# A spectral layer's sums and one residual pair moved to GpSimd, with the whole instruction order listed anew

## The chip, the cores and the metric

One NeuronCore of one Trainium2 chip runs the program. The metric is the time of one execution on the device, in microseconds (us). The engines are TensorE (PE in the rows), VectorE (DVE), ScalarE (ACT), GpSimd (POOL) and SyncE (SP), which issues most of the DMAs.

## The reference

The input is x, 2048 rows of 512 numbers. Four blocks follow one another, and each adds to x what it computes from the normalized x.

```python
def _A_ref(x, w_r, w_i):
    X = rfft2(x, axes=(-2, -1)) * (w_r + 1j * w_i)
    return irfft2(X, s=(S, D), axes=(-2, -1))

def _B_ref(x, w_gate, w_up, w_down):
    return ((x @ w_gate) * (x @ w_up)) @ w_down      # 512 -> 1792 -> 512

x = x + _A_ref(_layernorm(x), w_r, w_i)              # layer 0, spectral
x = x + _B_ref(_layernorm(x), w_gate, w_up, w_down)  # layer 0, GLU
x = x + _A_ref(_layernorm(x), w_r, w_i)              # layer 1, spectral
x = x + _B_ref(_layernorm(x), w_gate, w_up, w_down)  # layer 1, GLU
```

## The kernel before

x stays in SBUF as `xs`, 16 tiles of 128 rows by 512 columns. Fourier transforms are matrix products on TensorE, and so are the transposes. The GLU's products run in a rounded fp32 format (fp32r in the rows): each operand is a high part, which ScalarE copies, and a low part, what the copy lost, which mostly GpSimd subtracts.

**Spectral layer.** `fwd` (line 556) normalizes a tile, transposes it (`tp`), transforms the columns (`dp`) and begins the rows (`sp`), and ScalarE writes the result into E. `middle` (line 636) works through 16 groups of 512 spectral numbers. For a group VectorE transposes E into T, TensorE finishes the row transform (`zp`), ScalarE makes the rotated copy `jz` in two halves, VectorE multiplies `zp` by the real weights, GpSimd multiplies `jz` by the imaginary weights, somebody adds the two products into `ys`, TensorE begins the way back (`yp`), ScalarE copies into T, and VectorE transposes back into E. The tuples PE_ADDS and POOL_ADDS (lines 71 and 72, one entry for each layer) say who adds: in groups 2, 6, 8, 10 and 14 TensorE, which multiplies both products and accumulates; in all the others VectorE, from PSUM.

`inv` (line 717) brings a tile back: TensorE computes `vp` in two halves, ScalarE copies it to `vs`, TensorE computes `yi`, and the residual is added to xs. In the mode "plain" VectorE does that from PSUM in one pass of 512 columns and two of 256. MODES (line 79) gives one mode for each of the first four pairs of tiles, (0, 4), (1, 5), (2, 6) and (3, 7).

**Crossing to the GLU.** After both tiles of a pair have their statistics, ScalarE normalizes them (`xn`), TensorE transposes them (`tq`), and `build_x` (line 787) makes the seven left operands: XA, three blocks, and XS, four sums of blocks. For the first and third pair VectorE makes the sums; for the second and fourth GpSimd does, four subtractions or additions on the scratch `sx` or `sw`. The four low parts of XS are GpSimd's for every pair. The first products of the GLU (`unit`, line 932) are made over the first two pairs alone: `gw`, `gx`, `gy`, `gx`, `gz`, `gv`, `gz`; `gw` reads the first XS block, `gy` the second, `gz` the third, `gv` the fourth.

**GLU.** `unit` makes seven products for each of 14 column blocks of the weights, and `down` (products `ex` to `ev`) or `db` brings them back to 512 columns and into xs. From the second half of layer 0 on, the weights come from DRAM through DMAs that GpSimd issues (`kept_weights`, line 854: `wt<-gu`).

**Order.** Nothing is emitted where the code stands. Each instruction is first recorded by `plan.op`, which numbers it; `Plan.order` then sorts all of them, and they are emitted in that order, with each engine keeping it (`tc.keep_in_program_order`, in the helper that all rows name as line 411). So an engine takes its instructions strictly in the planned order, and one that waits holds up what stands behind it. Before the change, a list scheduler (`run`) picked by due times, and 277 stored random draws (MOVES) shifted these due times. `Plan.order` also says which buffer of a ring a tile gets.

Of the kernel before, what the change touches and what calls it, by code (L numbers as in the profile page):

```python
# [26 lines left out]
def consts():  # L27
# [44 lines left out]
POOL_ADDS = (), ()  # L72
# [6 lines left out]
MODES = ("plain", "plain", "plain", "fold"), ("plain", "plain", "plain", "fold")  # L79
# [6 lines left out]
MOVES = (  # L86
# [32 lines left out]
RATE = 270.0  # L119
WARM = 2  # L120
EARLY = 0
HOLD, FAR = {"DVE": 1.0, "ACT": 1.0, "POOL": 1.0}, 15.0
CLEAR = 1.5
FREE = ("a", "f", "st", "s1", "s2", "s3")
LOOK, SLACK = 0.08, 20.0
SLOTS = 5
WOVEN, WEND = 8, 20
STO, FRM = 10, 10
DOWNS8 = (7, 8, 11, 12, 15, 16, 19, 20)
DOWNS4 = (8, 12, 16, 20)  # L130
# [18 lines left out]
class Draw:  # L149
# [12 lines left out]
    def one(self, of):  # L162
        return of[int(self.part() * len(of))]
# [1113 lines left out]
```

## Time and profile before

| | us |
|---|---|
| median of 3 runs | 1087.72 (1087.59 to 1087.82) |
| the profiled execution | 1087.75 |
| its span, first to last instruction | 1086.0 |
| TensorE busy in the span | 1072.3 |
| VectorE, GpSimd, ScalarE busy | 841.1, 731.8, 457.7 |
| granted TensorE clock, mean | 1.000 |

Matmuls are pipelined and their ends are modelled, so a matmul's length in a row overlaps the next one; the distance from start to start is what TensorE takes for it.

### The profile page before, as it was taken

The numbers are of one execution on the slowest core, as the hardware profiler recorded it, in microseconds if no ns is written. First come the engines' busy times: TensorE is split into PE (matmuls) and PEld (weight loads), VectorE is DVE, ScalarE is ACT, GpSimd is POOL, SyncE is SP. The second block draws the span as 40 slices with busy tenths as digits, with TensorE's granted clock in tenths as the row PEclk, the third lists the DMA queues.
The fourth block names the chain that finished last, engine by engine and source line by source line (L and its number), as shares of the span: only waits on it lengthen the run. The fifth ranks groups of instructions, "written<-read, shape, count | busy, mean of one in ns | idle before, by whom it ended". The sixth has DMA issues, their size and how long they took to land.

```text
span 1086.0 us, 18629 instructions
## 1 busy us (share of the span) xinstructions
PE 1072.3 (99%) x6500; PEld 923.2 (85%) x6500; DVE 841.1 (77%) x1684; ACT 457.7 (42%) x1045; POOL 731.8 (67%) x940
## 2 busy tenths in 40 slices
PE   8999999999999999999999999999999999999998
PEld 6748988888899988888996489889989998888887
DVE  8597877777877875766897979777897876677778
ACT  6787643344542323323347775223442521223231
POOL 7396799978898666456674527466656984667771
PEclk9999999999999999999999999999999999999999
DMA  7665267556563457454454312655456256556542
GB/s 282 234 213 175 64 223 242 199 204 203 214 223 117 166 182 235 155 165 147 136 199 151 136 54 103 207 168 180 155 175 204 69 175 242 186 184 203 194 137 78
DMA packets 50301, 189.49 MB, mean 174 GB/s; under 512 B 5280, under 2 KB 19104, under 8 KB 39200
## 3 DMA queue, kind: packets, MB, share of 16 engines
q0 software_dynamic: 16128, 102.77, 28.8%
q1 hardware_dynamic: 33792, 85.01, 22.2%
q8 instruction: 52, 0.85, 0.3%
q10 hardware_dynamic: 288, 0.52, 0.1%
q14 instruction: 41, 0.34, 0.1%
HBM read 145.56 MB, written 42.73 MB: 173 GB/s over the span
## 4 chain that ended last, share of the span: by engine, by line
PE 89%; DVE 5%; issue 2%; ACT 2%; POOL 1%; DMA 0%; DVEq 0%; POOLq 0%; ACTq 0%
PE gx L411 14%; PE gz L411 14%; PE db L411 7%; PE gw L411 7%; PE gv L411 7%; PE gy L411 7%; PE ex L411 5%; PE ez L411 5%; PE yi L411 3%; PE ey L411 3%; PE ew L411 3%; PE ev L411 3%; PE sp L411 2%; PE dp L411 2%; PE vp L411 2%
## 5 line engine op out<-in xcount | busy, mean ns | idle before, releaser
L411 PE MATMUL gx<-xA,wt 128*128 128x512 f32 (+1 forms) x852 | 180.8, 347 | 0.0
L411 PEld LDWEIGHTS gx<-xA,wt 128*128 128x128 f32 x852 | 136.9, 190 | 17.2 <-ACT s L411 0.2
L411 DVE TENSOR_TENSOR q<-gy,s 128x512 f32<-128x512 f32 (+1 forms) x71 | 41.1, 578 | 73.4 <-PE gy L411 55.9
L411 ACT CAST sf<-q 128x256 fp32r<-128x256 f32 x99 | 40.2, 406 | 136.5 <-DVE q L411 84.0
L411 POOL TENSOR_TENSOR sf<-q,sf 128x256 fp32r<-128x256 f32 x99 | 73.6, 745 | 31.8 <-ACT sf L411 28.1
L411 DVE TENSOR_TENSOR xs<-xs,db 128x512 f32<-128x512 f32 x128 | 85.6, 683 | 11.4 <-PE db L411 11.0
L411 PE MATMUL db<-wd,h 128*128 128x512 f32 x336 | 91.1, 395 | 0.0
L411 POOL DMA_DIRECT2D wt<-gu x72 | 40.3, 560 | 74.7 <-PE gz L411 48.1
L411 PE MATMUL gz<-xA,wt 128*128 128x512 f32 (+1 forms) x426 | 90.1, 347 | 0.0
L411 PE MATMUL gw<-xS,wt 128*128 128x512 f32 (+1 forms) x426 | 90.0, 347 | 0.0
L411 PE MATMUL gv<-xS,wt 128*128 128x512 f32 (+1 forms) x426 | 90.0, 347 | 0.0
L411 PE MATMUL gz<-xS,wt 128*128 128x512 f32 (+1 forms) x426 | 89.8, 346 | 0.0
L411 PE MATMUL gy<-xS,wt 128*128 128x512 f32 (+1 forms) x426 | 89.7, 346 | 0.0
L411 POOL TENSOR_TENSOR sf<-cc,sf 128x256 fp32r<-128x256 f32 x99 | 73.2, 740 | 21.1 <-ACT sf L411 20.7
L411 PEld LDWEIGHTS gz<-xA,wt 128*128 128x128 f32 x426 | 69.1, 189 | 9.4
L411 PEld LDWEIGHTS gw<-xS,wt 128*128 128x128 f32 x426 | 68.8, 189 | 9.3 <-issue 0.3
L411 PEld LDWEIGHTS gy<-xS,wt 128*128 128x128 f32 x426 | 68.7, 190 | 9.0 <-issue 0.3
L411 PEld LDWEIGHTS gz<-xS,wt 128*128 128x128 f32 x426 | 68.8, 190 | 8.9
L411 PEld LDWEIGHTS gv<-xS,wt 128*128 128x128 f32 x426 | 68.5, 190 | 8.9 <-issue 0.3
L411 ACT COPY s<-gx 128x512 f32<-128x512 f32 (+1 forms) x71 | 35.3, 497 | 92.7 <-PE gx L411 80.7
L411 PEld LDWEIGHTS db<-wd,h 128*128 128x128 f32 x336 | 60.3, 189 | 10.3
L411 ACT CAST sf<-cc 128x256 fp32r<-128x256 f32 x99 | 40.1, 405 | 66.4 <-PE ez L411 22.3
(171 smaller groups left out, 2667.1 us busy)
## 6 DMA issues: line engine op xcount, KB each, us to landing
wt<-gu POOLq DMA_DIRECT2D x36, 1024.0 KB, 5.3
wt<-gu POOLq DMA_DIRECT2D x36, 768.0 KB, 4.7
bf<-dn POOLq DMA_DIRECT2D x20, 1024.0 KB, 5.5
bf<-dn POOLq DMA_DIRECT2D x20, 768.0 KB, 4.6
gu<-wt SPq DMA_DIRECT2D x14, 1024.0 KB, 6.9
gu<-wt SPq DMA_DIRECT2D x14, 768.0 KB, 3.5
wq<-in_wf_dram SPq DMA_DIRECT2D x10, 1024.0 KB, 6.1
rg<-in_wb_dram SPq DMA_DIRECT2D x14, 512.0 KB, 4.8
```

The lines of the kernel that those rows point to most:

```text
L411: ins = f(*args, **kw)
```

## The change

Two settings of layer 1 change. In groups 5, 9 and 13 of `middle` the two products are added by GpSimd: VectorE writes its product to SBUF instead of PSUM, and a GpSimd pass of 512 columns takes the place of one on VectorE. For the third pair (tiles 2 and 6) the mode is "pool": ScalarE copies `yi` to SBUF (`yc`), and GpSimd adds it to xs in four passes of 256 columns for each tile, in place of VectorE's three. TensorE's instructions stay the same 1200 blocks.

The scheduler with its draws is gone. A list ORDER of all 5057 instruction numbers gives the order; `Plan.order` walks it, and only keeps account of buffers. The order differs from the old one on every engine but the two first ScalarE loads, in both layers.

Numbers of the list used here. Layer 0: 603, 601 are the transposes (`tq`) of the second pair, 605 to 608 ScalarE's copies of them, 609 to 612 GpSimd's sums; 551, 549 the transposes of the first pair; 637, 627, 679, 847 are column transforms (`yi`); 844, 845, 878, 879, 857, 858 row transforms (`vp`) of later tiles; 736, 735 the GLU's first `gx` and `gw`. Layer 1: 2961, 2999, 3038 are the three sums of `middle`; 3146, 3144 the transposes of the second pair, 3149, 3150 ScalarE's first copies of them, 3152 to 3155 GpSimd's sums, 3159, 3161, 3163, 3165 the low parts of that pair's four XS blocks, 3105, 3107, 3109, 3111 those of the first pair; 3182 and 3170 are `yi` of tiles 6 and 2, 3183 and 3171 the copies `yc`, 3184 to 3187 and 3172 to 3175 the GpSimd passes; 3284, 3287 the first `gw` and `gy`; 3590, 3591 weight fetches of the third column block. Start: 5, 7, 8 are loads of x, 24 and 42 of row tables.

```diff
-POOL_ADDS = (), ()
+POOL_ADDS = (), (5, 9, 13)
...
-MODES = ("plain", "plain", "plain", "fold"), ("plain", "plain", "plain", "fold")
+MODES = ("plain", "plain", "plain", "fold"), ("plain", "plain", "pool", "fold")
...
-MOVES = (
-    1200000011, 1200000042, 1200000094, 1200000106, 1200000108, 1200000117, 1200000161, 1200000172, 1200000175,
...
+ORDER = (
+    0, 6, 5, 24, 42, 4, 7, 15, 1, 60, 78, 8, 9, 10, 13, 2, 11, 25, 18, 26, 3, 19, 20, 27, 43, 21, 36, 22, 44, 28, 23,
...
+    521, 592, 539, 693, 593, 694, 327, 597, 594, 326, 598, 329, 599, 595, 676, 596, 602, 522, 677, 600, 695, 603, 328,
+    523, 696, 678, 601, 605, 524, 634, 606, 697, 635, 607, 877, 525, 608, 625, 609, 698, 604, 624, 856, 526, 636, 610,
+    614, 679, 330, 613, 540, 615, 611, 541, 637, 619, 542, 545, 626, 616, 546, 547, 543, 680, 544, 617, 620, 681, 550,
+    627, 682, 618, 638, 548, 1087, 331, 612, 683, 699, 513, 639, 551, 621, 684, 700, 549, 640, 622, 701, 516, 628, 844,
+    552, 685, 845, 554, 629, 500, 553, 878, 501, 502, 555, 641, 890, 911, 879, 630, 556, 561, 857, 642, 559, 846, 562,
+    858, 565, 560, 736, 557, 880, 566, 702, 643, 735, 703, 558, 686, 737, 1034, 847, 563, 644, 567, 687, 645, 704, 564,
+    631, 741, 859, 632, 705, 568, 738, 848, 709, 706, 646, 710, 707, 647, 711, 708, 881, 651, 648, 714, 739, 652, 649,
+    860, 712, 1157, 650, 740, 715, 653, 849, 742, 656, 850, 1210, 851, 718, 744, 719, 743, 717, 852, 713, 721, 747, 745,
...
+    2958, 2977, 2987, 2952, 2959, 2943, 2978, 2970, 2915, 2953, 2988, 2960, 3003, 2994, 2979, 2971, 2961, 3021, 3022,
+    3033, 2996, 3011, 2980, 2995, 2989, 3050, 3034, 2962, 2997, 3035, 2923, 2990, 2998, 2981, 3036, 2963, 2933, 2999,
+    3004, 2944, 2991, 3042, 3037, 3012, 2964, 3005, 3023, 2972, 3014, 3038, 3006, 3043, 3013, 2954, 3024, 3051, 3007,
...
+    3075, 3135, 3180, 3136, 3064, 3076, 3181, 3427, 3140, 3077, 3141, 3078, 3142, 3137, 3138, 3167, 3139, 3145, 3065,
+    3168, 3079, 3143, 3223, 3081, 3066, 3224, 3448, 3067, 3169, 3146, 3068, 3080, 3182, 3069, 3149, 3150, 3082, 3083,
+    3225, 3152, 3144, 3084, 3183, 3239, 3088, 3089, 3151, 3090, 3184, 3085, 3086, 3170, 3093, 3087, 3153, 3240, 3158,
+    3241, 3185, 3091, 3226, 3242, 3186, 3148, 3243, 3171, 3162, 3157, 3187, 3227, 3415, 3244, 3147, 3172, 3094, 3228,
+    3188, 3245, 3416, 3229, 3173, 3449, 3097, 3156, 3246, 3174, 3450, 3230, 3092, 3189, 3247, 3154, 3249, 3417, 3191,
+    3231, 3095, 3175, 3098, 3418, 3160, 3232, 3102, 3104, 3155, 3248, 3428, 3099, 3159, 3429, 3164, 3100, 3285, 3190,
+    3250, 3163, 3101, 3233, 3106, 3161, 3110, 3192, 3286, 3234, 3096, 3176, 3105, 3251, 3290, 3430, 3103, 3107, 3252,
+    3177, 3284, 3193, 3256, 3108, 3111, 3257, 3287, 3194, 3258, 3253, 3419, 3254, 3261, 3109, 3255, 3198, 3431, 3199,
+    3259, 3200, 3195, 3165, 3288, 3262, 3196, 3289, 3203, 3291, 3197, 3420, 3265, 3293, 3421, 3266, 3201, 3292, 3268,
...
+    3334, 3321, 3323, 3359, 3441, 3361, 3453, 3325, 3360, 3335, 3336, 3379, 3590, 3326, 3362, 3328, 3364, 3327, 3442,
+    3363, 3330, 3337, 3365, 3324, 3445, 3443, 3446, 3367, 3331, 3444, 3447, 3454, 3366, 3338, 3591, 3455, 3368, 3329,
...
     def order(self, hop=0.12):
 
-        ops = self.ops
+        ops, out, rings, free, bus, port = self.ops, [], {}, {}, 0.75, 0.0
...
-        out, marks = self.run([], [])
-        for n in MOVES:
-            out, marks = self.run(out, *self.move(n, out, marks)[:1])
-        return out
...
+        for o in (ops[n] for n in ORDER):
+            e = o["e"]
+            at = max([self.after_(ops[p], o) for p in o["pre"]] + [free.get(e, 0.75), port if o["two"] else 0.0])
```

The branches that the two settings choose stand in the kernel already:

```python
                elif where == "POOL":
                    pool(512, lambda q=q, y=y: gtt(y(), y(), q(), ALU.add), [y, (q, 0), (q, 1)], [y])
...
        if mode == "pool":
            yc = temp("yc", "f")
            act(512, lambda: A.copy(yc(), yi()), [yi], [yc])
            y4 = lambda: yc().rearrange("p (b a d) -> p b a d", a=2, b=2)
            for b in range(2):
                pool(256, lambda b=b: gtt(xt[:, b], xt[:, b], y4()[:, 0], ALU.add), [yc, x_], [x_], due=due)
                pool(256, lambda b=b: gtt(xt[:, b], xt[:, b], y4()[:, 1], (ALU.add, ALU.subtract)[b]), [yc, x_], [x_])
```

## Rows read from the trace of the kernel before

**Rows 1.** The page, busy time of TensorE's matmuls, share of the span, instructions
```profile
PE 1072.3 (99%) x6500; PEld 923.2 (85%) x6500; DVE 841.1 (77%) x1684; ACT 457.7 (42%) x1045; POOL 731.8 (67%) x940
```

**Rows 2.** The page, the chain that ended last, by engine
```profile
PE 89%; DVE 5%; issue 2%; ACT 2%; POOL 1%; DMA 0%; DVEq 0%; POOLq 0%; ACTq 0%
```

**Rows 3.** Windows: stretch, then length and busy time of each engine (instructions), clock, DMA
```profile
0.00:60.00 60.00, 55.10 (x359) 39.77 (x360) 43.34 (x127) 42.37 (x105) 32.64 (x47) 1.00 0.71 251
...
90.00:130.00 40.00, 38.41 (x282) 36.08 (x282) 35.20 (x108) 32.34 (x87) 24.01 (x33) 1.00 0.33 113
130.00:556.00 426.00, 426.00 (x2498) 374.07 (x2498) 318.75 (x599) 152.25 (x331) 320.55 (x386) 1.00 0.55 185
...
600.00:620.00 20.00, 20.00 (x48) 8.66 (x47) 20.00 (x35) 15.84 (x28) 13.07 (x12) 1.00 0.31 104
620.00:650.00 30.00, 28.62 (x181) 24.94 (x180) 23.96 (x68) 20.53 (x54) 6.38 (x9) 1.00 0.20 65
...
680.00:1086.00 406.00, 401.89 (x2513) 362.42 (x2511) 309.57 (x538) 123.82 (x281) 256.23 (x359) 1.00 0.52 171
```

**Rows 4.** Timeline of TensorE, 570:680: start, length, instructions, [idle before, releaser]
```profile
589.78 3.70 PE L411 MATMUL zp<-T,midt 128*128 128x512 f32 x8 [0.62 <-DVE T L411]
...
624.90 2.18 PE L411 MATMUL vp<-tw,E 128*128 128x128 f32 x16 [0.28 <-DVE E L411]
...
637.98 1.06 PE L411 MATMUL yi<-di,vs 128*128 128x128 f32 x8
638.88 0.60 PE L411 MATMUL tq<-ident,xn 128*128 128x128 f32 x4
...
641.09 3.72 PE L411 MATMUL yi<-di,vs 128*128 128x256 f32 x16 [0.68 <-ACT vs L411]
645.23 0.66 PE L411 MATMUL tq<-ident,xn 128*128 128x128 f32 x4 [0.42 <-ACT xn L411]
...
651.61 0.96 PE L411 MATMUL gy<-xS,wt 128*128 128x256 f32 x6
...
653.13 1.05 PE L411 MATMUL yi<-di,vs 128*128 128x128 f32 x8
653.93 0.96 PE L411 MATMUL gz<-xS,wt 128*128 128x256 f32 x6
...
655.09 0.96 PE L411 MATMUL gv<-xS,wt 128*128 128x256 f32 x6
...
678.93 1.32 PE L411 MATMUL gw<-xS,wt 128*128 128x512 f32 x5
```

**Rows 5.** Groups of VectorE (DVE) in 585:660: busy, mean ns, idle before
```profile
L411 DVE TENSOR_TENSOR ys<-zp,jz 128x512 f32<-128x512 f32 x11 | 7.3, 666 | 0.0
L411 DVE TENSOR_TENSOR xs<-xs,yi 128x256 f32<-128x256 f32 x18 | 7.2, 415 | 0.1
L411 DVE TENSOR_TENSOR xs<-xs,yi 128x512 f32<-128x512 f32 x9 | 6.1, 682 | 4.3 <-PE yi L411 4.2
```

**Rows 6.** The tile jz on GpSimd (POOL), 585:625: ns min/median/max, first and last start
```profile
L411 POOL TENSOR_TENSOR jz<-jz,wr x8: 1266/1271/1277, 597.6 to 612.1; 128x512 f32<-128x512 f32 x8
```

**Rows 7.** Timeline of GpSimd, 586:700
```profile
643.17 3.15 POOL L411 TENSOR_TENSOR sw<-sw 128x256 f32<-128x256 f32 x4 [23.61 <-issue]
...
648.61 2.82 POOL L411 TENSOR_TENSOR xS<-sw,xS 128x256 fp32r<-128x256 f32 x4 [0.22 <-ACT xS L411]
...
667.40 0.59 POOL L411 DMA_DIRECT2D wt<-gu  x1 [0.54 <-PE gy L411]
```

**Rows 8.** Groups of ScalarE (ACT) in 620:655
```profile
L411 ACT COPY vs<-vp 128x512 f32<-128x512 f32 x11 | 6.1, 586 | 2.1 <-PE vp L411 2.1
```

**Rows 9.** Timeline of TensorE, 70:140
```profile
104.36 0.66 PE L411 MATMUL tq<-ident,xn 128*128 128x128 f32 x4 [1.16 <-ACT xn L411]
...
109.71 1.16 PE L411 MATMUL yi<-di,vs 128*128 128x128 f32 x8 [0.43 <-ACT vs L411]
```

**Rows 10.** Timeline of GpSimd, 60:125
```profile
103.73 3.15 POOL L411 TENSOR_TENSOR sx<-sx 128x256 f32<-128x256 f32 x4 [8.52 <-ACT sx L411]
```

More of the change, by code (lines that the diff above doesn't have):

```diff
@@ L121 @@
 EARLY = 0
-HOLD, FAR = {"DVE": 1.0, "ACT": 1.0, "POOL": 1.0}, 15.0
 CLEAR = 1.5
-FREE = ("a", "f", "st", "s1", "s2", "s3")
-LOOK, SLACK = 0.08, 20.0
 SLOTS = 5
@@ L146, in __call__ @@
         return self.tile
-class Draw:
-    def __init__(self, seed):
-        self.at = seed * 0x9E3779B97F4A7C15 % 2 ** 64
-    def part(self):
-        self.at = (self.at + 0x9E3779B97F4A7C15) % 2 ** 64
-        z = self.at
-        z = (z ^ z >> 30) * 0xBF58476D1CE4E5B9 % 2 ** 64
-        z = (z ^ z >> 27) * 0x94D049BB133111EB % 2 ** 64
-        return ((z ^ z >> 31) >> 11) * 2.0 ** -53
-    def one(self, of):
-        return of[int(self.part() * len(of))]
-    def bell(self):
-        return (self.part() + self.part() + self.part() + self.part() - 2.0) * 1.7320508
 class Plan:
@@ L174 @@
              **{f"{r}{p}": n for p in range(4) for r, n in (("s", SLOTS),)}}
-    FREE = FREE
     def __init__(self):
@@ L213, in order @@
             o["due"] = d - 1.1 * o["lag"] - hop - 0.3 * (o["e"] == "PE")
-        self.kinds = [(o["e"], *(t.name for t in o["tiles"])) for o in ops]
-        out, marks = self.run([], [])
-        for n in MOVES:
-            out, marks = self.run(out, *self.move(n, out, marks)[:1])
-        return out
-    def move(self, n, out, marks):
-        ops, draw = self.ops, Draw(n)
-        end = max(o["end"] for o in out)
-        lo, span = -20.0 + draw.part() * (end + 10.0), draw.one((10.0, 20.0, 40.0, 80.0, 160.0))
-        share, jit, way = draw.one((0.0, 0.25, 0.5, 1.0)), draw.one((0.0, 0.0, 2.0, 5.0)), draw.part()
-        inside = [o for o in ops if lo < o["start"] < lo + span]
-        if way < 0.4 and inside:
-            kind, by = self.kinds[draw.one(inside)["i"]], 8.0 * draw.bell()
-            for o in inside:
-                if self.kinds[o["i"]] == kind:
-                    o["due"] += by
-        elif way < 0.7 and inside:
-            for _ in range(1 + int(3.0 * draw.part())):
-                draw.one(inside)["due"] += 8.0 * draw.bell()
-        elif inside:
-            self.latest(out, end)
-            shifts = sorted(o["late"] - o["due"] for o in inside)
-            shift = shifts[len(shifts) // 2]
-            for o in inside:
-                o["due"] += share * (o["late"] - shift - o["due"]) + jit * draw.bell()
-        return [m for m in marks if m[1] < lo - 15.0], lo + span
@@ L244, in latest @@
-    def latest(self, out, end):
-        ops = self.ops
-        nxt, two = {}, None
-        for o in reversed(out):
-            long = o["end"] - o["start"]
-            late = end - long
-            for s in o["suc"]:
-                late = min(late, ops[s]["late"] - (0.0 if ops[s]["next_to"] is o else long))
-            if o["e"] in nxt:
-                late = min(late, nxt[o["e"]] - o["pitch"])
-            if o["two"]:
-                if two is not None:
-                    late = min(late, two - o["pitch"])
-                two = late
-            for t in o["tiles"]:
-                if t in self.after:
-                    late = min(late, self.after[t]["late"] - long)
-            nxt[o["e"]] = late
-            o["late"] = late
+        for o in ops:
+            for t in o["tiles"]:
+                t.left, t.slot, t.freed = t.users, None, 0.0
@@ new lines, in order @@
+        for o in (ops[n] for n in ORDER):
+            e = o["e"]
+            at = max([self.after_(ops[p], o) for p in o["pre"]] + [free.get(e, 0.75), port if o["two"] else 0.0])
+            if e == "SP":
+                at = max(at, o["due"] - o["ahead"])
+            for t in o["tiles"]:
+                if t.slot is None:
+                    t.slot = True
+                    q = rings.setdefault(t.ring, [])
+                    t.index = len(q)
+                    if len(q) == self.RINGS.get(t.ring, 1):
+                        old = min((u for u in q if not u.left), key=lambda u: u.freed)
+                        at = max(at, old.freed)
+                        q.remove(old)
+                        t.index = old.index
+                    q.append(t)
+            o["start"] = at
+            free[e] = at + o["pitch"]
+            if o["two"]:
+                port = at + o["pitch"]
+            if o["kb"]:
+                bus = max(bus, at) + o["kb"] / RATE
+                o["end"] = max(at + o["lag"], bus + 2.3)
+            else:
+                o["end"] = at + o["lag"] + hop + 0.3 * (e == "PE")
+            for t in o["tiles"]:
+                t.left -= 1
+                t.freed = max(t.freed, o["end"])
+            out.append(o)
```

104 lines of the change are left out of this document (removed), and 264 rows, old and new, of tables (MOVES, ORDER).

## The prediction

> **What bounds the kernel now.** I read the page's busy times first, then its chain, then windows by stage, then the timelines where windows leave TensorE idle. The reader should see in [rows 1] that TensorE is busy for 1072.3 of 1086.0 us, and in [rows 2] that 89% of the chain that ended last is TensorE's own work. The change removes no work from TensorE, so it can gain only what TensorE waits. The windows place these waits [rows 3]: 4.9 us in the first 60, 1.6 in 90 to 130 where layer 0 crosses from its spectral part to the GLU, none in 130 to 556, 1.4 in 620 to 650 where layer 1 crosses, and 4.1 after 680, most of it the tail of additions and stores after the last product. Between 680 and the tail TensorE does not wait, so what is gained or lost before 680 arrives at the end in full.
>
> In layer 1 two things stand side by side. From 600 to 620 VectorE is busy 20.00 of 20 us, and so is TensorE [rows 3]; relief for VectorE alone is worth only the small holes of TensorE. And at the crossing TensorE stops three times, 0.28, 0.68 and 0.42 us, on VectorE's transpose, ScalarE's copy and ScalarE's normalizing [rows 4]. GpSimd, which gets the work, stood still for 23.61 us until 643.17 [rows 7]. In layer 0 the same crossing has stops of 1.16 and 0.43 us [rows 9], and GpSimd begins its sums at 103.73 after 8.52 us of nothing [rows 10].
>
> The sum below is made against the profiled execution, 1087.75 us (span 1086.0 and 1.75 around it); the median, 1087.72, is the same within the spread.
>
> **1. Three sums in layer 1's middle.** Removed from VectorE: 3 passes of 0.666 us [rows 5], about 0.6 from start to start, so 1.8. Added to GpSimd: 3 passes; a product of the same shape takes 1.27 us [rows 6], so 3.8 in a stretch where GpSimd worked 13.07 of 20 [rows 3]. ScalarE is not touched. What does it buy? TensorE's stretch from the first `zp` at 589.78 to the stop at 624.90 [rows 4] lasts 35.1 us. Its own work there is 16 `zp`, 16 `yp` and 5 second `yp`, 37 blocks; 8 instructions in 3.70 us put a block of two at about 0.86, 31.8 in all; with four `vp` blocks of 0.5 (16 instructions in 2.18) and the small product, 33.9. So 1.2 us are waiting. VectorE, full throughout, would end 1.8 us sooner, TensorE can end 1.2 sooner at best. I take 1.0, as the first turns of the stage are not helped; bounds 0 (GpSimd's sums, in series behind its products, come late) and 1.2. **-1.0**
>
> Does moving work from VectorE to GpSimd slow either? [Rows 6] shows GpSimd's products at 1.266 to 1.277 us in the stretch where VectorE was full, so in that traffic neither blocked the other. The Trainium skill has a rule against such a change: Perfetto Trace Analysis, "Optimizing Scalar/DVE Operations", says that the two share an SBUF read port, so that moving work between them might not help. SBUF — State Buffer, "Who interferes with whom", narrows it to VectorE instructions with two SBUF inputs, which VectorE's work here mostly isn't (one input is in PSUM). By the row the sum stands; by the first rule terms 1 and 2 would be zero.
>
> **2. The third pair on GpSimd, and layer 1's crossing.** VectorE loses, for two tiles, one pass of 0.682 and two of 0.415 each [rows 5], 3.0 us by duration, some 2.5 from start to start. ScalarE gains two copies of 0.586 [rows 8], 1.2 us, in a window where it has 9.5 free [rows 3]. GpSimd gains 8 passes; four of that shape took 2.82 us, 0.70 each [rows 7], 5.6 in all. Behind them in GpSimd's queue stand the low parts that the GLU's first products need. In the new list I count the GpSimd instructions from 3152: `gw` needs 3105, the 16th, `gy` 3107, the 17th, and the last low part, 3165, is the 20th; before, they were 12.
>
> When can 3152 start? It started at 643.17 because ScalarE made its copies late. The list puts 3149 and 3150 right behind the transposes; the earlier one ran at 637.98 + 0.90 = 638.88 at the latest [rows 4], so some 639. After it GpSimd waits for tile 6: `yi` 1.8 us (half of 3.72 [rows 4]), the copy 0.59, so about 641. From there 16 instructions of 0.70 to 3107: 652.1, and 1.0 less for term 1: 651.1. `gy` started at 651.61 before [rows 4]. Without its stops TensorE would be there some two us sooner, so GpSimd, not VectorE, sets this point, and only 0.3 to 0.5 us come on top of term 1. I take 0.3. Bounds: a gain of 1.1 (both later stops gone), a loss if 3152 cannot start early (the slow rival). **-0.3**
>
> The weight fetch 3590 stood 24 instructions behind 3152 and was issued at 667.40 [rows 7]; it now stands 40 behind. 40 of 0.70 are 28 us: 667 from a start at 639, perhaps 671 with waits, landing some 5 us later (the queue's median on the page). TensorE needs it at 678.93 [rows 4], or about 677.5 now. That covers it by a little; I take nothing, bound 3 us of loss.
>
> **3. Layer 0's crossing, order alone.** Before, the transpose that waited 1.16 us for its normalized tile stood ahead of `yi` 627, and `yi` 847 waited 0.43 [rows 9]. In the list 603 and 601 come before the last `vp` blocks, ScalarE's copies 605 to 608 directly behind, 637 and 627 ahead of 551 and 549 together, six `vp` blocks after these, and 847 behind the first `gx` and `gw`. So 1.8 us of ready work fills the first stop, the second loses its place, and GpSimd's sums, which set the low parts, can start perhaps 1.5 us before 103.73 [rows 10]. The two stops are 1.6 us; I take 1.5; bounds 0 and 2.0. **-1.5**
>
> **4. Everything else in the order.** The first 60 us have 4.9 us idle [rows 3], of which the first load and the first statistics are no matter of order. The list also sends loads 24 and 42, 128 KB each, ahead of load 7; 256 KB at the 251 GB/s of that window [rows 3] is 1.0 us by which tiles 2 and 3 can be late. Gain bound 2.5, loss bound 1.0. I take 0.8 over all other stages, since the list moves blocks at nearly every small hole I looked at. **-0.8**
>
> **5. Kinds of neighbours on TensorE.** A `yi` block of 8 took 0.90 us when a fp32 transpose followed (637.98 to 638.88) and 0.80 when a fp32r product followed (653.13 to 653.93) [rows 4]. The list has, net, nine fewer short blocks (`tp`, `yi`, `vp`, `tq`) followed by fp32r: 9 × 0.09 = 0.8. Some stand where TensorE waits anyway; I take 0.6; bounds 0 and 0.9. **+0.6**
>
> Sum: 1087.75 - 1.0 - 0.3 - 1.5 - 0.8 + 0.6 = 1084.75, so **1084.8 us**, 0.27% faster.
>
> **Rivals.**
>
> *The gains don't add up (no measurable change).* In both crossings GpSimd's low parts take over as what ends last; the holes merely move. For it: GpSimd's chain grows from 12 to 20 instructions, and in layer 0 it is as long as before. Then terms 1 to 3 give perhaps 1.4 together, terms 4 and 5 cancel: 1086.4. The shared-port rule ends in the same place: terms 1 and 2 gone, 1086.1.
>
> *Slower: GpSimd's chain starts no earlier than before.* If the copies ahead of 3152 still wait for VectorE, 3152 starts at 643.17; at the 0.79 of the four sums there (3.15 us [rows 7]) 17 instructions end at 656.6, 5.0 us after the old `gy`. Term 1 is lost too: 1087.75 + 5.0 - 1.5 - 0.8 + 0.6 = 1091.1. It begins to cost from a start of about 640 on, and outweighs the rest from about 642. Against it: GpSimd's long rest, and the list's order on ScalarE. A fetch 3590 that lands after 678 is the same mechanism one stage later.
>
> *More than forecast.* The new order removes most of what is removable: both stops of layer 0, all three of layer 1 and 2.5 at the start: 1087.75 - 1.2 - 1.1 - 2.0 - 2.5 + 0.4 = 1081.4.
>
> **Chances.** A measurement of this kernel tells 0.2%, 2.2 us, from no change. The forecast case, 2.2 to 4.5 us faster, 0.45; more than that 0.10; within 2.2 us 0.33; slower by more 0.12. So faster 0.55, same 0.33, slower 0.12. The range leaves out some 0.06 below and 0.13 above: **1082.0 to 1089.0**. The likeliest case alone is 1083.3 to 1085.5.
>
> **What would show it.** Right: VectorE still full in the middle but ended about 1.8 us sooner, the first `yi` of layer 1 about 1 us sooner; GpSimd at work from about 639 on, its low parts ending just ahead of `gw` and `gy`; no stop of over 0.5 us between 100 and 112; TensorE's busy blocks 1200 as before; DVE instructions 9 fewer. Wrong: TensorE waiting on GpSimd's `xS` at `gw` or `gy`, or on a DMA at the third column block; a stop of tile 2's transpose in the first 12 us; or new holes between 680 and 1080, where today there are none and where the order was changed as well.

## The result, and the profile after

The changed kernel took 1091.07 us (median of 8 runs, 1089.40 to 1091.59), the kernel before on the same chip 1087.92 (8 runs, 1087.26 to 1088.80). The ratio is 1.0025, with a 95% interval of 1.0015 to 1.0036: slower by about a quarter of a per cent. Forecast were 1084.8 and a range of 1082.0 to 1089.0; the time lies above it. The profiled execution took 1090.86 us, its span is 1089.1, the mean granted clock 0.998. Five of the eight executions have that mean clock and took 1090.86 to 1091.59; the three with 0.999 or 1.000 took 1089.40 to 1089.84, which is above the range too.

The page of after, busy times and chain, answers to [rows 1, 2]:

```profile
PE 1074.9 (99%) x6500; PEld 925.9 (85%) x6500; DVE 837.4 (77%) x1675; ACT 458.1 (42%) x1047; POOL 741.6 (68%) x951
...
PE 80%; POOL 7%; DVE 3%; issue 2%; ACT 2%; DMA 0%; POOLq 0%; DVEq 0%; ACTq 0%
```

Nine DVE instructions went, eleven came to GpSimd, as announced. TensorE is busy 2.6 us longer with the same 6500 matmuls, and the chain leads through GpSimd for 7% of the span, before for 1%. The windows, in the order of [rows 3]:

```profile
0.00:60.00 60.00, 54.46 (x351) 40.11 (x352) 40.53 (x122) 40.75 (x99) 30.13 (x44) 0.97 0.67 243
90.00:130.00 40.00, 39.70 (x289) 37.50 (x288) 35.24 (x108) 34.81 (x94) 26.89 (x36) 1.00 0.50 168
130.00:556.00 426.00, 424.79 (x2476) 372.37 (x2475) 316.60 (x593) 151.49 (x330) 320.66 (x387) 1.00 0.54 185
600.00:620.00 20.00, 19.82 (x46) 8.38 (x45) 20.00 (x36) 15.88 (x31) 16.89 (x16) 1.00 0.37 131
620.00:650.00 30.00, 29.80 (x175) 24.77 (x173) 22.31 (x59) 21.31 (x53) 10.09 (x15) 1.00 0.24 75
680.00:1089.10 409.10, 404.90 (x2532) 365.11 (x2531) 311.63 (x543) 123.49 (x282) 257.42 (x361) 1.00 0.52 171
```

The two windows of the crossings are nearly free of TensorE's waits now (0.30 of 40 and 0.20 of 30 us, against 1.6 and 1.4; layer 1's has moved out of its window in part, see below), and GpSimd took up the work of layer 1 (16.89 us busy from 600 to 620 against 13.07). What the windows show as new: eight matmuls fewer in the first 60 us, a clock of 0.97 there, and 1.2 us of waiting in 130 to 556, where there was none.

A window does not say when time is lost, since its edges are fixed. For that, the start of TensorE's n-th matmul is taken from both traces; the difference is how late the changed kernel is at that point. Matmuls are counted from 0. Where the order of blocks differs locally, a single value can be off by up to 1 us: it is 1.17 at no. 1380 and 0.24 at no. 1400, though nothing is gained between; where both run like blocks it is steady, 1.30 from 1000 to 1140 and 2.33 at 1560, 1580, 1620 and 1640. Layer 0's start ends ahead of no. 500, its crossing lies between 500 and 700, layer 1's middle between 3400 and 3600, its crossing between 3600 and 3900.

| TensorE's matmul no. | 300 | 500 | 700 | 1400 | 1600 | 3000 | 3400 | 3600 | 3900 | last |
|---|---|---|---|---|---|---|---|---|---|---|
| starts before, us | 45.7 | 97.9 | 125.6 | 267.3 | 306.3 | 529.1 | 578.2 | 626.7 | 668.8 | 1081.5 |
| changed kernel, late by | 2.02 | 3.14 | 1.01 | 0.24 | 2.66 | 2.36 | 3.34 | 2.93 | 2.80 | 3.10 |

So the loss comes ahead of layer 1's middle: 3.1 us at the start, 1.35 between nos. 700 and 3000 (1.0 of it between the steady values), 1.0 between 3000 and 3400. The crossing of layer 0 gave back 2.1 (1.8 by the steady value behind it). Layer 1, where GpSimd's new work is, gained 0.4 in its middle; the 0.1 at its crossing is less than a single value can tell. Each place can be seen in timelines. TensorE's waits between 9 and 60 us, then the first of them as it was before:

```profile
9.01 1.33 PE L487 MATMUL dp<-df,fs 128*128 128x128 f32 x8 [1.41 <-DVE fs L487]
31.87 1.16 PE L487 MATMUL dp<-df,fs 128*128 128x128 f32 x8 [0.64 <-DVE fs L487]
52.63 2.84 PE L487 MATMUL zp<-T,midt 128*128 128x512 f32 x6 [1.58 <-DVE T L487]
58.66 1.55 PE L487 MATMUL yp<-ys,midt 128*128 128x512 f32 x3 [0.38 <-DVE ys L487]
```

```profile
8.61 1.16 PE L411 MATMUL dp<-df,fs 128*128 128x128 f32 x8 [1.07 <-DVE fs L411]
```

The first line waits for VectorE's `fs`, and on VectorE a statistic of the next tile waits for its load ahead of that `fs`; the load stands behind two tables in SP's queue and is issued at 2.12 us. Before, it stood ahead of them (the last line here), and the statistic did not wait:

```profile
2.12 0.43 SPq L487 DMA_DIRECT2D xs<-in_x_dram  x1
...
7.93 0.69 DVE L487 BATCH_NORM_STATS2 st<-xs 128x6 f32<-128x512 f32 x1 [0.84 <-DMA xs<-in_x_dram]
8.54 0.41 DVE L487 TENSOR_TENSOR fs<-tp,fb 128x256 f32<-128x256 f32 x1
...
0.75 0.86 SPq L411 DMA_DIRECT2D xs<-in_x_dram  x2
```

The wait is only 0.34 us longer than before. But behind it TensorE's granted clock falls from 2.4 to 1.2 GHz for 3.4 us (0.50 in the third column from the right); before, it stood at 1.00 there (the last line), and 25 matmuls ran in the 3 us instead of 16:

```profile
9.00:10.00 1.00, 0.99 (x8) 0.99 (x9) 0.96 (x5) 0.00 (x0) 1.00 (x2) 0.93 0.95 344
10.00:13.00 3.00, 3.00 (x16) 2.77 (x17) 2.96 (x12) 1.84 (x7) 3.00 (x5) 0.50 1.03 414
13.00:14.00 1.00, 1.00 (x8) 0.70 (x8) 0.96 (x4) 0.68 (x1) 0.96 (x2) 0.86 1.01 414
...
10.00:13.00 3.00, 3.00 (x25) 2.33 (x25) 2.96 (x8) 2.38 (x6) 2.68 (x5) 1.00 1.03 406
```

At 52.63 the first turn (the first transposes of E into T) is late. One reading: the list has ScalarE copy the second piece of E ahead of the rest of the first, and VectorE's transposes begin with one that reads both. The run first_turn, below, does not bear this out, and the cause inside the first turn stays open. Another candidate in the trace, which no run tries by itself: ScalarE's last two `us` of this stage start at 47.22 and 48.17 now and at 45.02 at the latest before, and the copies into E follow them. The same transposes began at 48.77 before, while TensorE still had row products (`sp`) to do (the last two lines):

```profile
50.04 1.43 ACT L487 COPY E<-sp 128x257 f32<-128x257 f32 x6 [0.20 <-PE sp L487]
...
51.28 1.90 DVE L487 STREAM_TRANSPOSE T<-E 128x512 f32<-128x512 f32 x3 [5.23 <-ACT E L487]
...
48.77 2.49 DVE L411 STREAM_TRANSPOSE T<-E 128x512 f32<-128x512 f32 x4 [8.91 <-ACT E L411]
...
48.57 0.92 PE L411 MATMUL sp<-us,tw 64*128 64x193 f32 x8 [0.40 <-ACT E L411]
```

At 273 us the rounded copies `u` of kept weights are stored to DRAM (`dn`) from two buffers of the ring that the GLU's temporaries use. The stores were issued at 258.68 before (the last line) and at 267.67 now, where they land 4.5 us after their issue; the next users of these buffers, a sum `c` on VectorE and `xn` on ScalarE, wait for them, and `gz` behind `c`:

```profile
267.67 1.02 SPq L487 DMA_DIRECT2D dn<-u  x2
...
272.30 0.69 DVE L487 TENSOR_TENSOR c<-gz,q 128x512 f32<-128x512 f32 x1 [1.85 <-DMA dn<-u]
...
273.04 1.20 PE L487 MATMUL gz<-xA,wt 128*128 128x512 f32 x4 [0.85 <-DVE c L487]
...
258.68 1.04 SPq L411 DMA_DIRECT2D dn<-u  x2
```

What is lost between nos. 3000 and 3400 is lost at one place: the kernel is 2.25 us late at no. 3060 and 3.22 at 3080. VectorE's `q` waits 1.38 us there for GpSimd's `cc`, and two products of TensorE wait behind VectorE. Each wait reads 0.18, but from the start of the matmul ahead to the start of the second one behind it pass 0.68 and 0.65 us, where two others take 0.24; that is 0.85 of the 0.98.

```profile
538.69 0.43 DVE L487 TENSOR_TENSOR q<-gy,s 128x256 f32<-128x256 f32 x1 [1.38 <-POOL cc L487]
...
539.17 0.98 PE L487 MATMUL gz<-xS,wt 128*128 128x256 f32 x6 [0.18 <-DVE q L487]
540.32 0.95 PE L487 MATMUL ez<-bf,sf 128*128 128x256 f32 x6 [0.18 <-DVE ew L487]
```

Layer 1 on TensorE, for [rows 4], and GpSimd, for [rows 7]:

```profile
593.29 4.56 PE L487 MATMUL zp<-T,midt 128*128 128x512 f32 x10 [0.63 <-DVE T L487]
...
626.03 3.98 PE L487 MATMUL vp<-tw,E 128*128 128x128 f32 x32
...
650.04 1.16 PE L487 MATMUL yi<-di,vs 128*128 128x128 f32 x8 [0.24 <-ACT vs L487]
...
653.73 0.98 PE L487 MATMUL gx<-xA,wt 128*128 128x256 f32 x6 [0.88 <-ACT s L487]
654.54 0.88 PE L487 MATMUL gw<-xS,wt 128*128 128x256 f32 x6
655.26 0.88 PE L487 MATMUL gy<-xS,wt 128*128 128x256 f32 x6
```

```profile
641.95 0.72 POOL L487 TENSOR_TENSOR sw<-sw 128x256 f32<-128x256 f32 x1 [18.87 <-issue]
...
651.36 5.62 POOL L487 TENSOR_TENSOR xS<-sw,xS 128x256 fp32r<-128x256 f32 x8
...
674.29 0.57 POOL L487 DMA_DIRECT2D wt<-gu  x1
```

The stretch from the first `zp` to the first `vp` takes 32.74 us. GpSimd's first sum starts at 641.95, which is 639 on the old clock of events (TensorE is 2.9 late there), as forecast. The stops of 0.68 and 0.42 us are gone; a new one of 0.88 came, of the second `gx` on a copy of the first.

### The profile page after: what moved, and what is told of

Its sections match the earlier page's. It is cut to its first block, busy times and chain, and to the rows that moved or that the text cites. A ratio compares the mean times of both kernels' runs of the same rounds, so it can differ in the third digit from the quotient of the medians.

```text
span 1089.1 us, 18620 instructions
## 1 busy us (share of the span) xinstructions
PE 1074.9 (99%) x6500; PEld 925.9 (85%) x6500; DVE 837.4 (77%) x1675; ACT 458.1 (42%) x1047; POOL 741.6 (68%) x951
## 4 chain that ended last, share of the span: by engine, by line
PE 80%; POOL 7%; DVE 3%; issue 2%; ACT 2%; DMA 0%; POOLq 0%; DVEq 0%; ACTq 0%
PE gx L487 13%; PE gz L487 13%; PE gy L487 7%; PE gv L487 6%; PE gw L487 6%; PE db L487 5%; PE ex L487 5%; PE ez L487 5%; PE ey L487 3%; PE ev L487 3%; PE yi L487 2%; PE ew L487 2%; PE yp L487 2%; PE vp L487 2%; POOL wt L487 2%
```

## The experiments

OLD is the list of the kernel before in the new numbers, with the added GpSimd work where the replaced instructions stood; NEW is the changed list. `OLD[:k] + NEW` means OLD's first k entries, then all others in NEW's order. Every kernel but old_settings has the changed settings. Times are medians, with the median of the kernel before beside them and the ratio's 95% interval.

**The halves.** What belongs to layer 1, and what to the settings?

```diff
-ORDER = NEW
+ORDER = OLD[:2900] + NEW   # layer1_new: layer 0 as before
+ORDER = OLD                # old_order_new_settings
```

> Old order up to layer 1's first transpose E to T (2900 instructions), from there on the changed kernel. Theory A: the middle of layer 1 gains about 0.5 us and nothing is lost before it: about 1087.4 (1086.8 to 1088.0). Theory B: 1089.5 or more.

> The two settings alone, with the old order of all instructions (a GpSimd pass stands where the VectorE pass stood). Theory A: the settings cost little, 1087.5 to 1089. Theory B: GpSimd's passes delay the low parts of layer 1's crossing, 1090 or more, with TensorE waiting for xS near 651.

layer1_new took 1087.20 against 1087.63 (0.9988 to 1.0005): the 3 us are gone, so they came from the order of the first 2900 entries, which is all that differs. A gain over the kernel before is not clear of noise. old_order_new_settings took 1095.62 against 1087.63 (1.0058 to 1.0084). With the old order GpSimd's passes stand where VectorE's did, `gw` waits for its low part, and the clock falls with it, to 0.50 for 6.8 us:

```profile
656.67 1.44 PE L490 MATMUL gw<-xS,wt 128*128 128x256 f32 x5 [4.25 <-POOL xS L490]
```

The opposite kernel has the new order without the new GpSimd work:

```diff
-POOL_ADDS = (), (5, 9, 13)
+POOL_ADDS = (), ()
-MODES = ("plain", "plain", "plain", "fold"), ("plain", "plain", "pool", "fold")
+MODES = ("plain", "plain", "plain", "fold"), ("plain", "plain", "plain", "fold")
```

> The changed list with what GpSimd does anew undone: the three sums back on VectorE, the third pair's residual passes as before (the list less the operations that exist only in the new form). Theory A (the new GpSimd work gains 1.0 in layer 1's middle and nothing at its crossing): 0.6 to 1.6 us more than the changed kernel, 1091.7 to 1092.7. Rival B (it gains nothing, layer 1's 0.6 comes from the order): 1091.

1093.91 against 1087.81 (1.0046 to 1.0072), 2.8 us more than the changed kernel and more than either theory had. Its layer 1 has two stops that the changed one does not have (what ends the second, the profile does not show), and the one at the second `gx` takes 1.05 instead of 0.88:

```profile
617.93 1.12 PE L489 MATMUL zp<-T,midt 128*128 128x512 f32 x2 [1.17 <-DVE ys L489]
649.90 0.71 PE L489 MATMUL vp<-tw,E 128*128 128x128 f32 x4 [2.43 <-issue]
656.79 0.97 PE L489 MATMUL gx<-xA,wt 128*128 128x256 f32 x6 [1.05 <-ACT s L489]
```

**The start.**

```diff
-ORDER = NEW
+ORDER = OLD[:302] + NEW               # start_old
+ORDER = OLD[:335] + NEW               # start_old_all
+ORDER = OLD[:395] + NEW               # start_old_395
+ORDER = NEW[:395] + OLD[:2900] + NEW  # start_new
```

> The changed kernel with its first 302 instructions (all up to layer 0's first transpose E to T) in the old order, the rest as changed. Theory A (the loss is made in the first 50 us by the new order there): TensorE's first zp comes at about 49.5 again instead of 52.6, the granted clock does not fall after it has risen, and the time is about 1088.0, within 0.1% of the kernel before. Theory B (GpSimd's added work in layer 1 makes the loss): still 1090 or more.

> The first 335 entries of the list in the order of the kernel before (all loads, all of stage 1's start, the first turns and zp matmuls), the rest as changed. Theory A: no lateness at 50 us and the clock at 1.000 throughout; left are +1.5 at 272 us (waits for a store's buffer), +0.9 at 540 us, -2 at layer 0's crossing and -0.6 in layer 1's middle, so about 1088.0 (1087.2 to 1088.8). Rival B (the lateness comes from all of layer 0's order and the splice only moves it): 1089.5 to 1091.5. Rival C (GpSimd in layer 1): 1091.

> The first 395 entries in the order of the kernel before, all the rest as changed; at this place the two lists differ by three operations only (at the cuts of start_old and start_old_all by more of the turns' work). Theory A: nothing lost up to 65 us, 2 us gained at layer 0's crossing, 1.5 lost at 272 us, 0.9 at 540 us, 0.6 gained in layer 1: 1087.6 (1087.0 to 1088.3). Rival B (the changed list behind 65 us needs its own start, whatever the cut): a wait of about 2 us at a zp or yp product between 50 and 80 us once more and 1090 to 1091.2.

> The first 395 entries of the list as changed (loads, stage 1 and the first turns of layer 0, up to about 65 us), the rest of layer 0 in the order of the kernel before, layer 1 as changed: against layer1_new only the start differs, and the two lists hold the same work up to this place but for three operations. Theory A (the new start itself costs the time): TensorE is 2.5 to 3.5 us late at 65 us, this is not caught up, and the time is 1089.3 to 1090.7. Rival B (what is lost at the start is caught up at the waits of layer 0's crossing): 1087.4 as layer1_new.

start_old and start_old_all took 1090.96 and 1091.07: misses. Both are on time at no. 300, and then TensorE waits 1.97 us at the first `zp` (51.43) and 2.19 at a `yp` (60.50), with a fall of the clock behind each. Both cuts lie in the middle of the turns. The texts above speak of more work that differs there, but it is not more: what the two lists hold up to the cut differs by two operations at 302, by five at 335 and by three at 395. What makes the first two cuts so dear is not shown. start_old_395 took 1089.41 against 1087.76 (1.0006 to 1.0023), 1.5 us better than the changed kernel but outside both theories; a wait of 1.06 us is left at 66 us. start_new, the same part put into the good kernel, took 1091.35 (1.0020 to 1.0042), 3.6 us above its kernel before, where layer1_new was 0.4 below: the start by itself makes more than the whole difference that was measured. So the parts do not add up: put into the good kernel the start costs 4.0 us, taken out of the changed one it gives 1.5.

Which part of the start?

```diff
-ORDER = NEW
+ORDER = OLD[:53] + NEW               # loads_old
+ORDER = NEW[:53] + OLD[:2900] + NEW  # loads_new
...
-    281, 291, 295, 296, 292, 293, 379, 333, 350, 517, 341, 358, 351, 368, 342, 334, 359, 389, 343, 399, 352, 335, 369,
+    ... 280, 281, 291, 259, 293, 292, 294, 350, 333, 351, 296, 295, 358, 341, 379, 352, ...   # first_turn
```

> The changed list with its first 53 entries alone (the first loads and the first work on them, to about 10 us) in the order of the kernel before; both lists hold the same 53 there. Theory A (the order of the loads and the first turn each cost their own): the wait ahead of the first dp is 1.07 us as before, the clock stays at 1.000, TensorE is not late at 45 us, the wait of 1.6 us at the first zp is still there, and the time is 1.0 to 2.0 us less than the changed kernel, about 1089.5. Rival B (what the loads cost is waited for anyway at the first zp): that wait grows to over 2.5 us and the time stays at 1091.

> The kernel layer1_new with the first 53 entries alone in the changed order. Theory A: TensorE 0.6 to 2.0 us late at 45 us, not caught up, 1088.2 to 1089.5. Rival B (the old first turn takes the lateness up): as layer1_new, 1087.4.

> The changed kernel's list with only entries 294 to 320 put into the relative order that they had before: the stage-1 pieces of the first group and the first two turns (333, 350) come ahead of the second piece's copies (295, 296) and of turn 379. Theory A (the new order of layer 0's start causes the loss, in two places: the first matmuls and the first turn): the TensorE wait of about 1.6 us ahead of the first zp matmul is gone, so 1.1 to 1.9 us less than the changed kernel, about 1089.5. Rival B (the wait at the first zp is only where lateness of the loads shows): the wait comes back at another matmul before 70 us and the time stays at about 1091. Rival C (GpSimd's work in layer 1 costs the time): no difference, 1091.

loads_old took 1089.33 against 1087.81 (1.0009 to 1.0027): the wait ahead of the first `dp` is back at 1.07 us, the clock stays at 1.00, and the 1.58 us at the first `zp` remain. So loads and first turn each cost their own in the changed kernel. loads_new took 1087.57 (0.9989 to 1.0007), 0.2 us below its kernel before against 0.4 for layer1_new, a miss for theory A: in the old order the new loads cost 0.9 us of TensorE's time at no. 500 in the profiled run, in which the clock fell, and hardly anything in the median. The wait of 0.46 us at 16 us that the old order has takes part of the lateness up; and the executions differ, 1086.55 to 1087.25 us at a mean clock of 1.000 and 1087.57 to 1089.70 at 0.998 or less. first_turn took 1091.09, a miss: in its profiled run the same loads landed later (a wait of 2.31 us ahead of the first `dp`), and the 1.58 us became 0.91 at `zp` and 0.67 at `yp`. From no. 300 to 500, behind the loads, it loses 1.08 us and the changed kernel 1.12. So putting the entries 294 to 320 back moved the wait and did not reduce the loss.

**The clock.** One product of 128x512 more on TensorE in the hole ahead of the first `dp`; the reference does not have it, and nothing reads it.

```diff
+            if fill:
+                TE.matmul(wp(), warm()[:, 0:128], warm(), start=True, stop=True)
```

> The changed kernel with one more warm-up product (128x512, its result is read by nothing) on TensorE behind tile 1's turns at the start of layer 0, in the 1.4 us in which TensorE waits ahead of the first dp: work that the reference does not have, for the clock alone. Theory A (part of the loss is the fall of the granted clock at 9.9 to 13.3 us): the clock stays at 1.000 in every run, and the time is 1.3 to 1.7 us less than the changed kernel, about 1089.5. Rival B: the clock falls all the same, then or elsewhere, or the time before 13 us was set by the loads whatever the clock, and the time stays at 1090.7 to 1091.3.

1090.24 against 1087.60 (1.0015 to 1.0035). The clock stays at 1.00 there in the profiled run, and no execution has a mean clock below 0.999:

```profile
10.00:13.00 3.00, 3.00 (x27) 2.50 (x26) 2.96 (x10) 2.36 (x7) 3.00 (x4) 1.00 1.02 416
```

27 matmuls ran in 3 us, 16 in the changed kernel. With the two added matmuls counted off, TensorE is 0.8 us less late at no. 300, and 0.4 at the end. The first `dp` itself started 0.48 later (9.49), since the load that it hangs on came 0.48 later in this execution (VectorE's statistic starts at 8.41, in the changed kernel at 7.93). The gain in the median is half of what was expected, and the interval does not separate it from none.

**The middle of layer 0, and the best combination.**

```diff
-ORDER = NEW
+ORDER = NEW[:1308] + OLD[:1700] + NEW                        # mid_old
+ORDER = OLD[:302] + NEW[:886] + OLD[:2900] + NEW             # pieces
+ORDER = OLD[:395] + NEW[:1168] + OLD[:2900] + NEW            # combined
+ORDER = OLD[:491] + NEW[:1168] + OLD[:2900] + NEW            # combined_late
```

> The changed list with its entries 1308 to 1700 alone (layer 0, about 238 to 318 us) put back into the order of the kernel before. Theory A (the copies u of a spectral group's coefficients come so late there that their buffers are still being stored when c and xn want them): the TensorE wait of 0.85 us at 273 us and the drift of 1.1 to 1.7 us there are gone, and the time is 1.0 to 1.6 us less than the changed kernel: 1089.6. Rival B: the wait comes back at the next use of the same buffers, 1091.

> Old order in the first 302 instructions, new order through layer 0's middle and crossing (to TensorE's block 165), old order from there to layer 1's first transpose, new order after it. Theory A: it keeps the 2.2 us that layer 0's crossing gained and the 0.5 us of layer 1 and leaves the start's loss and the two new stops near 272 and 539 out: about 1085.5 (1084.8 to 1086.5). Theory B: 1088 or more.

> Old order up to entry 395, the changed order from there to entry 1168 (layer 0's crossing, to about 208 us), the old order for the rest of layer 0, the changed order for layer 1. Theory A (gains at the two crossings and in layer 1's middle, losses at the start, at 272 and at 540 us only): 1085.2 (1084.5 to 1086.0), faster than both kernels. Rival B (each cut leaves a wait of its own): 1086.5 to 1090.

> As the kernel combined, with the old order up to entry 491 instead of 395 (about 82 us), still ahead of layer 0's crossing. Theory A (the wait of 1.05 us at 66 us belongs to the cut): it is gone, nothing takes its place, and the time is about 1.0 us less than combined, 1085.8. Rival B: the crossing's gain of 2 us needs the changed order from 65 us on, and the time is 1087 or more.

mid_old took 1090.24 against 1087.76 (1.0014 to 1.0032). The wait at 273 is gone and did not come back; from no. 700 to 3000 it loses 0.23 us where the changed kernel loses 1.35. In the median this is 0.7 us of the 1.0 to 1.6 that were expected, and the intervals overlap; in its profiled run the first loads came later still (2.56 us of waiting ahead of the first `dp`). pieces, 1091.70, missed: it has start_old's cut, and its second cut left four more waits between 145 and 167 us. combined took 1086.80 against 1087.76 (0.9981 to 0.9998), combined_late 1086.49 against 1087.81 (0.9978 to 0.9995). Both miss what theory A forecast, but both are faster than the kernel before, by 0.1%, and combined_late is some 4.5 us below the changed kernel; the two are not clear of each other. In combined_late the wait at 66 us is gone, but one of 1.07 us at the `vp` of 86.04 (0.48 in combined) takes most of its place.

**Layer 1's new stop.**

```diff
-    ... 3105, 3251, 3290, 3430, 3103, 3107, 3252, 3177, 3284, 3193, 3256, 3108, 3111, 3257, 3287, ...
+    ... 3105, 3251, 3430, 3103, 3107, 3252, 3177, 3284, 3193, 3256, 3108, 3111, 3257, 3287, 3290, ...
```

> Layer 0 in the order of the kernel before, layer 1 as changed (the kernel layer1_new), with one matmul moved: the second gx product (3290) stands behind gy (3287), not directly behind the first gx. Theory A: the wait of 0.88 us at the second gx product (for the copy of the first) is gone and nothing else takes its place, so 0.8 to 1.0 us less than layer1_new: 1086.3. Rival B: the copy of the first gx is late for other work on its engine anyway, the wait moves to the next product and the time stays at 1087.2.

1087.60 against 1087.60 (0.9992 to 1.0010), nothing gained. With `gx` out of the way, `gw` waits for GpSimd's low part:

```profile
648.77 0.28 PE L490 MATMUL gw<-xS,wt 128*128 128x256 f32 x1
650.32 0.86 PE L490 MATMUL gw<-xS,wt 128*128 128x256 f32 x5 [1.26 <-POOL xS L490]
```

The copy of `gx` was only the last of two things that were late; GpSimd's chain bounds this place.

How late TensorE is in the kernels that decide, by their profiled runs:

| late by, at matmul no. | 300 | 500 | 700 | 1400 | 1600 | 3000 | 3400 | 3600 | 3900 | last |
|---|---|---|---|---|---|---|---|---|---|---|
| changed kernel | 2.02 | 3.14 | 1.01 | 0.24 | 2.66 | 2.36 | 3.34 | 2.93 | 2.80 | 3.10 |
| layer1_new | -0.30 | -0.29 | -0.29 | -0.29 | -0.29 | -0.37 | -0.38 | -0.96 | -1.07 | -0.75 |
| old_order_new_settings | 0.02 | 0.02 | 0.02 | 0.02 | 0.02 | 0.58 | 0.59 | 1.44 | 8.21 | 8.21 |
| old_settings | 1.08 | 2.19 | 0.06 | -0.71 | 1.67 | 1.37 | 2.32 | 3.59 | 5.86 | 6.15 |
| start_new | 0.98 | 2.94 | 2.86 | 2.86 | 2.86 | 2.85 | 2.83 | 2.25 | 2.14 | 2.43 |
| loads_old | 0.37 | 1.50 | -0.63 | -1.28 | 1.12 | 0.84 | 1.80 | 1.38 | 1.26 | 1.56 |
| loads_new | 0.59 | 0.58 | 0.48 | 0.48 | 0.47 | 0.41 | 0.41 | -0.17 | -0.30 | 0.16 |
| mid_old | 2.80 | 3.93 | 1.80 | 1.99 | 1.99 | 2.03 | 3.03 | 2.60 | 2.48 | 2.78 |
| combined_late | -0.02 | 0.97 | -1.16 | -0.86 | -0.86 | -0.92 | -0.93 | -1.51 | -1.67 | -1.37 |

## Why the prediction was wrong

**The step that failed is term 4, "everything else in the order".** It took a gain of 0.8 us and a loss of 1.0 at most. Measured along the table: +3.14 up to no. 500, +1.35 from 700 to 3000, +0.98 to 3400, a loss of 5.5. With 5.5 in its place the sum gives 1091.05, close to the 1091.07 measured, but in part by luck: term 1 is 0.6 too large and term 3 0.6 too small. It is luck as well that the slower rival's 1091.1 is the time that came: its mechanism, a late start of GpSimd's chain in layer 1, did not happen. Three things were wrong in term 4.

- The start. The late tile was seen, and put at 1.0 us. TensorE was 2.0 late by no. 300, 1.65 more than in loads_old, as the wait was followed by a fall of the clock that the term did not have. What the fall costs can be estimated from two runs in which the load came at nearly the same time (statistic at 8.49 and 8.41): first_turn, with the fall, is 2.62 late at no. 300, fill, without it, 1.25, so some 1.3. At the end loads_old is 1.5 (trace) and 1.6 us (medians) below the changed kernel.
- The first turn, a wait of 1.58 us at the first `zp` and 1.1 us of lateness, was not seen: the list was not followed there through ScalarE's work to VectorE's first transpose. loads_old shows that it is no matter of the loads; which entries make it stays open (first_turn).
- "None in 130 to 556" was read as nothing to gain, and a loss was not looked for. A stretch without waits has none to give back. The order around the buffer that is still being stored costs 1.1 us there (1.35 against 0.23 in mid_old), of which the wait itself is 0.85. What costs 1.0 between nos. 3000 and 3400 was not tried by itself: the trace places 0.85 of it at the two waits at 539 and 540, behind GpSimd's `cc`; OLD's order there is free of it (combined_late).

**Term 1** (-1.0 in layer 1's middle): right in kind, too large, measured -0.41 in the changed kernel and -0.58 in layer1_new. The stretch to the first `vp` took 32.74 us, without the four `vp` blocks of 0.5 that the term counted into its 35.1; the rest of the difference, some 0.4, is the gain. The 1.2 us of waiting were found by subtracting blocks at 0.86, and were not there: before, TensorE was busy for 34.72 of the 35.12 us, so it had 0.40 to give back, 0.28 of it the stop at `vp`; a block of two takes 0.88 us over the whole stretch. The stretch before and after:

```profile
589.78:624.90 35.12, 34.72 (x92) 16.01 (x92) 35.04 (x63) 25.37 (x45) 20.75 (x19) 1.00 0.34 120
...
593.29:626.03 32.74, 32.56 (x76) 14.21 (x77) 32.71 (x59) 24.51 (x44) 24.68 (x22) 1.00 0.35 124
```

With the old settings in the same order the middle lasts 1.7 longer (from no. 3400 to 3600, +1.27 against -0.41), most of it one stop of 1.17, so in this order the sums on GpSimd buy more than the term gave them.

**The port that the two engines share.** GpSimd's three sums took 1.270 to 1.280 us each in a stretch where VectorE was busy 20.00 of 20 us, as its products did before [rows 6], and VectorE's own sums took 0.659 us against 0.666 [rows 5]: neither engine was slowed. The Trainium skill (Perfetto Trace Analysis, "Optimizing Scalar/DVE Operations") says that the two share an SBUF read port, so that moving work between them might not help; the prediction took from it that terms 1 and 2 would be zero. The trace does not agree: no such sharing shows in these durations. That the two terms came out small has another reason: TensorE had little waiting to give back.

**Term 2** (-0.3 at the crossing): -0.13, small as forecast, and too small for its sign to be shown. The start of 3152 came out at 639, and the two later stops are gone. What TensorE stops for now is ScalarE's copy of `gx`, 0.88 us, which the term did not have; layer1_gx shows that GpSimd's chain, as the term said, sets the point next, 1.26 us. The fetch 3590 was in time. **The slower rival** was real as a mechanism: in the old order it costs 6.8 us (nos. 3600 to 3900 of old_order_new_settings). What avoids it is the new order of layer 1, so settings and order are worth nothing apart: alone they lose 7.6 and about 3.8 us behind no. 3400, together they gain 0.2 to 0.4 in the traces, which the medians do not separate from nothing.

**Term 3** (-1.5 at layer 0's crossing): -2.13, or -1.84 to the steady value of 1.30, at its upper bound of 2.0. combined_late shows the same, -2.13 and -1.83.

**Term 5** (+0.6 by neighbours on TensorE): TensorE is busy 1073.1 us in loads_old, whose clock does not fall at the start, 0.8 more than before. That neighbours make this is not shown; combined_late, with the changed order at both crossings, is busy 1071.7, 0.6 less than before.

Sum of the measured terms: -0.41 - 0.13 - 2.13 + 5.47 and +0.30 behind no. 3900 make +3.10, the lateness of the last matmul; what term 5 is worth lies inside these differences. The range failed for the same reason as the sum: it took the losses of an order from places where TensorE already waited.

## What to carry to other kernels

Where an order is replaced as a whole, follow the new list through the stretches that are full today, not only through the holes: each first use of a late load, each first reader of a piece that is written in parts, and each reuse of a buffer whose store is in flight. A gain in one stage and a loss in another are told apart by the start of the n-th matmul in both traces, and by swapping whole stretches of the list at places where both lists hold the same work: here the cuts where they hold exactly the same (at 53 and 2900) left no wait of their own, while cuts among the turns where they differ by two to five operations left 1.06 to 2.19 us. Relief for one engine and the order that uses it belong together, and are tried together.

## What the runs showed of the hardware

The granted clock fell to 1.2 GHz behind TensorE waits of 1.35 us (loads_new, at 8.84 us), 1.41 (the changed kernel), 1.97 (start_old), 2.19 (start_old_all), 2.31 (first_turn), 2.56 (mid_old) and during one of 4.25 (old_order_new_settings), and did not fall behind waits of 1.34 (fill), 1.50 (old_settings, 9.31), 1.76 (start_new, 9.22) and 2.43 (old_settings, 649.90). So the length of the wait alone does not tell. Each fall lasted 3.4 us, the last one 6.8.

What one fall at the start is worth is an estimate. The runs first_turn and fill give some 1.3 us by no. 300, as worked out above. In start_new the executions with a mean clock of 0.999 or 1.000 took 1090.19, 1090.31 and 1090.36 us, those with 0.997 or 0.998 took 1091.31 to 1091.97, 1.3 us more in the mean; in the changed kernel the same comparison gives 1.7. The mean clock alone does not say where a fall was: in the traces of fill and combined_late the clock falls only behind the last matmuls, where TensorE has nothing more to do, and in combined_late the executions with 0.998 took just 0.2 us more than those with 1.000.

And the landing of the same loads varied. In seven profiled runs of kernels with the same first 53 entries, VectorE's statistic of the second tile, which waits for its load, started at 7.77 (loads_new), 7.93 (the changed kernel), 8.15 (start_new), 8.24 (old_settings), 8.41 (fill), 8.49 (first_turn) and 8.68 us (mid_old): a spread of 0.9 us, as much as most terms of the forecast.
